# Attention beside a feed-forward network: the value products of a unit in one step or in two

## The chip, the cores and the metric

One core of one Trainium2 chip runs the whole program. The metric is the device time of one execution in microseconds. The engines are TensorE (PE, its weight loads PEld), VectorE (DVE), ScalarE (ACT) and GpSimd (POOL); SyncE (SP) issues the transfers by DMA.

## The reference, cut to what matters

```python
def _attn_ref(q, k, v, proj):                 # q, k, v: 4 x 8 x 768 x 64, proj: 64 x 6
    q_bits = (np.einsum('bhsd,dk->bhsk', q, proj) > 0)
    k_bits = (np.einsum('bhsd,dk->bhsk', k, proj) > 0)
    ...                                        # 6 bits make a bucket number
    mask = q_bucket[:, :, :, None] == k_bucket[:, :, None, :]
    scores = np.where(mask, scale * np.matmul(q, k.transpose(0, 1, 3, 2)), -1e9)
    attn = np.exp(scores - np.max(scores, axis=-1, keepdims=True))
    attn = attn / (np.sum(attn, axis=-1, keepdims=True) + 1e-09)
    return np.matmul(attn, v)

def _moe_ref(x, w_in, w_out):                 # x: 3072 x 512, 512 -> 2048 -> 512
    h = x @ w_in
    g = h * np.clip(h + 3.0, 0.0, 6.0) / 6.0
    return g @ w_out
```

The heads' outputs, laid side by side, are the tokens x of the feed-forward network (FFN).

## The kernel before, in words

Every product of 32-bit numbers is made of products of a rounded high part (fp32r) and of what is left of it, the low part. A high part is a cast by ScalarE; its low part is a subtraction by VectorE or GpSimd.

**Attention** goes by *row tiles*: tile k (0 to 191) holds 128 queries of one head against its 768 keys, six tiles to a head. For each, PE makes the scores (`lead`, L387 and L389: two banks of 384), VectorE takes the row minimum of the negated scores (`lowest`, L396), ScalarE the exponential with its row sum (`exponential`, L408). Two tiles make a *unit* u (tiles 2u and 2u+1). Up to tile 101 the probabilities are transposed by PE. From tile 102 (`GT`) on VectorE turns them inside blocks (`flip`, L429), a transfer writes them to DRAM (`fd<-p`), and four loads bring them back turned, two into a tile named `spare` and two into `px` (`move`, for tile k+1 at the end of step k; SP issues them). Then `split_p(k - 1, c)` makes the high part of a half c in tile ph and the low part in tile pl: ScalarE's cast L475 for both halves, GpSimd's subtraction L477 for c = 1, VectorE's L479 for c = 0. Row w = 0 of a unit's four tiles (ph and pl of c = 1 and of c = 0) is written in the odd step behind the tile, row w = 1 in the even step after. Tags ph and pl have two buffers each, and a unit takes both. The **value products** of a unit are twelve matmuls of 128x256 into one PSUM bank `acc`: six with the high parts, six with the low parts, of c = 1 first. `values_whole` (L513) makes them all at the start of an odd step. `output` then copies acc to a tile y (ScalarE, L547) in the next even step.

**The FFN** goes by chunks of 256 tokens, 16 places to a chunk, one place to a step. A generator `fill` makes it and is taken up four times in a step: A splits the gate's result (ScalarE's cast L689 and VectorE's L690), B makes the first layer (L661: eight products with x's high parts xh, four with its low parts xl), C makes the second layer of the place before (L699, L700, and as last the third terms L704, which need L690's result) and the gate (ScalarE L683, VectorE L684), D does side work: the reciprocals of the row sums (VectorE L567), the spreading of them (GpSimd L577), normalising transposes on PE (L587, into banks named rt), and at place 15 the split of the next chunk's x (L650 on ScalarE, L651 on VectorE).

**The hash** of a head ahead (`hash_qk`, L334 to L336) multiplies its queries and keys (high parts qq and kk, their low parts made by GpSimd in L318, which wait in a list `subs`; the transfers of the split wait in `moves`) into two PSUM banks z. VectorE reads the bits off them (`bits`, L352). Banks for z, h, acc and rt come from `bank`, in turn out of four.

The order on PE, VectorE, ScalarE and GpSimd is the order in which the code issues (a manual schedule); DMAs stand on SP's queue in that order too. From step 101 on one function, `beside_ffn`, writes a step. Its step k, before the change: in odd steps the value products of unit (k-3)/2; row minimum of tile k+2 (behind stage A where a hash was made in the step before); A; exponential and flip of tile k+2; split_p(k-1, 1); B; in even steps the copy of acc; in odd steps with (k+3) % 6 == 4 the hash of the next head; C, with split_p(k-1, 0) inside it; bits; scores of tile k+3; transfers; one low part of q or k from `subs` in odd steps; D.

Line numbers are those of the kernel before. In the changed kernel, lines from 516 on stand 15 lower for the parts named here (L661 becomes L676, L690 becomes L705, L547 becomes L562, L587 becomes L602), and L513 is in the new function `values_part`.

## Time and profile before

| | us |
|---|---|
| three runs | 974.35, 977.39, 976.26; median 976.26 |
| the profiled execution | 973.11, of it 971.3 in the span of the profile |
| mean granted clock of TensorE | 0.998 |
| busy share of the span | PE 98%, DVE 74%, ACT 64%, POOL 49% |
| stage 0 to 396 us: attention alone, row tiles 0 to about 100, weights split beside it | PE busy 385.3 of 396.0 |
| stage 396 to 813 us: attention beside the FFN, steps 101 to 192 | PE busy 410.2 of 417.0 |
| stage 813 to 971.3 us: the rest of the FFN | PE busy 152.6 of 158.3 |

Times are read from one profiled execution. A group's row gives line, engine, operation, output and input tiles, shape and count, then the busy time of all and the mean of one in ns, then the engine's idle time just before them and what ended most of it. A row of instructions in time gives start, duration, engine, line, tiles and (in brackets) the idle time in front and what ended it. A row by windows gives the stretch, its length and the busy time (and count) of PE, PEld, DVE, ACT and POOL, the granted clock, the share of the DMA engines and GB/s. Weight loads overlap the products; starts of PE's instructions are therefore better read than their ends.

### The profile page before, as it was taken

How to read it: one execution, taken by the hardware profiler on the slowest of the kernel's cores; microseconds unless marked ns; L12 is line 12 of the kernel's file. 1: busy time of each engine (PE TensorE's matmuls, PEld its weight loads, DVE VectorE, ACT ScalarE, POOL GpSimd, SP SyncE). 2: the span in 40 equal slices, each digit the busy share in tenths (PEclk: the TensorE clock that was granted, in tenths of full speed). 3: DMA queues.
4: the chain of work that ended last, by engine and by line, in shares of the span. 5: the costliest groups of instructions: out<-in, count | busy, mean ns of one | idle time of the engine just before them, and what ended most of it. 6: DMA issues, size and time to landing. Idle time of an engine off the chain costs nothing.

```text
span 971.3 us, 19460 instructions
## 1 busy us (share of the span) xinstructions
PE 948.0 (98%) x6306; PEld 873.6 (90%) x6306; DVE 723.5 (74%) x1470; ACT 625.0 (64%) x1421; POOL 473.6 (49%) x582
## 2 busy tenths in 40 slices
PE   8999999999999999899999999999999999999997
PEld 7999888999989999799899899989899899889896
DVE  7999988888569999877878878878777874342422
ACT  6898875655478988667766666666666664333332
POOL 6777744665537776455555545555545432000000
PEclk9999999999999999999999999999999999999999
DMA  3567579100035554787898788788887772101000
GB/s 117 140 156 188 131 224 377 58 1 1 6 119 119 115 142 112 192 252 233 238 267 234 231 256 241 230 267 236 243 258 233 211 227 71 44 1 44 1 22 22
DMA packets 113613, 152.06 MB, mean 157 GB/s; under 512 B 13876, under 2 KB 82612, under 8 KB 113512
## 3 DMA queue, kind: packets, MB, share of 16 engines
q1 hardware_dynamic: 108472, 144.79, 48.8%
q0 software_dynamic: 5040, 6.03, 5.3%
q8 instruction: 50, 0.82, 0.4%
q14 instruction: 51, 0.42, 0.2%
HBM read 77.34 MB, written 54.00 MB: 135 GB/s over the span
## 4 chain that ended last, share of the span: by engine, by line
PE 79%; DVE 8%; DMA 4%; ACT 4%; issue 3%; POOL 1%; SPq 1%; ACTq 0%; DVEq 0%; POOLq 0%
PE h L661 25%; PE acc L500 6%; PE po L704 6%; PE po L699 6%; PE po L700 6%; PE acc L513 6%; PE pt L418 5%; PE s L389 5%; PE s L387 5%; DMA spare<-fd 2%; DVE p L396 2%; DVE pl L479 2%; ACT ph L475 1%; SPq L78 1%; DVE qq L352 1%
## 5 line engine op out<-in xcount | busy, mean ns | idle before, releaser
L408 ACT ACTIVATE p<-p,m 128x768 f32<-128x768 f32 x192 | 180.2, 939 | 113.4 <-DVE p L396 105.2
L396 DVE TENSOR_SCALAR_CACHE_REDUCE p<-s 128x768 f32<-128x768 f32 x192 | 182.7, 952 | 24.9 <-PE pt L418 12.4
L684 DVE SCALAR_TENSOR_TENSOR h<-g,h 128x256 f32<-128x256 f32 x192 | 81.1, 423 | 102.0 <-ACT g L683 99.0
L683 ACT ACTIVATE g<-h,three 128x256 f32<-128x256 f32 x192 | 91.2, 475 | 94.9 <-PE h L661 94.0
L661 PE MATMUL h<-xh,w 128*128 128x256 f32 x1024 | 146.8, 282 | 0.0
L661 PEld LDWEIGHTS h<-xh,w 128*128 128x128 f32 x1024 | 134.9, 188 | 4.2 <-ACT xh L650 0.6
L429 DVE STREAM_TRANSPOSE p<-p 128x768 f32<-128x768 f32 x90 | 88.1, 979 | 65.2 <-ACT p L408 65.1
L477 POOL TENSOR_TENSOR pl<-spare,ph 128x384 fp32r<-128x384 f32 x45 | 45.8, 1018 | 127.3 <-ACT ph L475 71.4
L479 DVE TENSOR_TENSOR pl<-pt,ph 128x384 fp32r<-128x384 f32 x196 | 100.0, 550 | 4.0 <-ACT ph L475 3.5
L387 PE MATMUL s<-kk,qq 76*128 76x384 f32 x384 | 100.5, 343 | 2.0 <-ACT kk L357 1.5
L389 PE MATMUL s<-kk,qq 128*128 128x384 f32 x384 | 100.4, 343 | 0.0
L700 PE MATMUL po<-w,gb 128*128 128x512 f32 x250 | 98.4, 393 | 0.0
L699 PE MATMUL po<-w,gb 128*128 128x512 f32 x250 | 98.3, 393 | 0.0
L475 ACT CAST ph<-pt 128x384 fp32r<-128x384 f32 x196 | 86.1, 474 | 14.3 <-PE pt L418 13.0
L216 POOL TENSOR_TENSOR w<-wr,w 128x128 fp32r<-128x128 f32 x128 | 71.9, 593 | 45.2 <-ACT w L210 41.9
L418 PE MATMUL pt<-ident,p 128*128 128x128 f32 x612 | 86.2, 275 | 1.9 <-DVE pl L479 1.1
L689 ACT CAST gb<-h 128x256 fp32r<-128x256 f32 x141 | 52.4, 372 | 54.5 <-DVE h L684 26.8
L661 PE MATMUL h<-xl,w 128*128 128x256 f32 x512 | 81.2, 280 | 0.0
L418 PEld LDWEIGHTS pt<-ident,p 128*128 128x128 f32 x612 | 72.5, 141 | 8.9 <-PE pt L418 1.5
L704 PE MATMUL po<-w,gb 128*128 128x512 f32 x250 | 78.6, 395 | 1.5 <-DVE gb L690 1.5
L318 POOL TENSOR_TENSOR kk<-raw,qq 64x192 fp32r<-64x192 f32 (+1 forms) x73 | 65.4, 920 | 25.1 <-ACT qq L304 21.7
L387 PEld LDWEIGHTS s<-kk,qq 76*128 76x128 f32 x384 | 66.6, 190 | 11.7 <-ACT kk L357 2.0
(153 smaller groups left out, 2150.9 us busy)
## 6 DMA issues: line engine op xcount, KB each, us to landing
fd<-p SPq DMA_DIRECT2D x90, 384.0 KB
spare<-fd SPq DMA_DIRECT2D x180, 96.0 KB
px<-fd SPq DMA_DIRECT2D x180, 96.0 KB
kk<-qq SPq DMA_DIRECT2D x62, 192.0 KB
wr<-in_w_in SPq DMA_DIRECT2D x16, 512.0 KB
wr<-in_w_out SPq DMA_DIRECT2D x16, 512.0 KB
raw<-in_qkT SPq DMA_DIRECT2D x19, 384.0 KB
vr<-in_v SPq DMA_DIRECT2D x32, 192.0 KB
```

The source lines that it names most:

```text
L387: nc.tensor.matmul(s[:, c, :HW], lhsT=q1[:KM, us], rhs=half(k1[:KM], c), start=True, stop=False)
L389: nc.tensor.matmul(s[:, c, :HW], lhsT=q2[:, us], rhs=half(k2, c), start=False, stop=True)
L396: nc.vector.tensor_scalar(out=pr_[:], in0=s[:, :, :HW], scalar1=CAP, scalar2=None, op0=ALU.min, op1=ALU.min, accum_out=m[:],)
L408: nc.scalar.activation(pr_[:], pr_[:], AF.Exp, bias=m[:], scale=-1.0, accum_out=sms[b][:, t, h : h + 1])
L418: nc.tensor.transpose(pt[:, x], probs[g][0][:, c, x * P : (x + 1) * P], ident[:])
L475: nc.scalar.copy(hi, pt)
L479: lows.append(lambda: engine.tensor_sub(lo, pt, hi.bitcast(F32)))
L661: nc.tensor.matmul(hp, lhsT=wi[:, wp, wc], rhs=x[cc][xp], start=(k == 0 and cc == 0), stop=(k == 2 and cc == NCC - 1),)
L683: nc.scalar.activation(r[:], hp, AF.Relu, bias=three[:], scale=1.0)
L699: nc.tensor.matmul(po[u], lhsT=gh[:, us], rhs=wo[:, 0], start=(fc == 0), stop=False)
L700: nc.tensor.matmul(po[u], lhsT=gh[:, us], rhs=wo[:, 1], start=False, stop=False)
L704: nc.tensor.matmul(po[u], lhsT=gl[:, us], rhs=wo[:, 0], start=False, stop=(fc == NFC - 1))
```

## The change

The six high-part products of a unit stay in its odd step k, but stand behind the first layer (stage B); the six low-part products stand at the start of step k+1. The copy of acc stays in step k+1 at its place. The hash moves to the step before, an even one ((k+3) % 6 == 3), and whatever waits in `subs` and `moves` is issued ahead of it; `behind` follows it. A low part of q or k may now be issued in every step but those at place 15. The tiles, their buffers and the arithmetic stay.

```diff
+    def values_part(u: int, part: int):
+        vv = vvs[2 * u // KT]
+        if part == 0:
+            accs[u] = bank([P, 2 * P], f"acc{u}")
+        acc = accs[u]
+        for c in (1, 0):
+            y = parts[u, c][part]
+            for x in range(QT):
+                nc.tensor.matmul(
+                    acc[:], lhsT=vv[:, c * QT + x], rhs=y[:, x],
+                    start=(part, c, x) == (0, 1, 0), stop=(part, c, x) == (1, 0, QT - 1),
+                )
+            if part:
+                del parts[u, c]
...
+    begun_unit = None
+
+    def value_part(k: int, part: int):
+        nonlocal vnext, begun_unit
+        u = vnext // 2
+        if part == 0 and u < NS // 2 and 2 * u >= GT and k % 2 and k >= 2 * u + 3:
+            values_part(u, 0)
+            begun_unit = u
+        elif part == 1 and begun_unit is not None:
+            values_part(begun_unit, 1)
+            through.append(begun_unit)
+            begun_unit = None
+            vnext += 2
...
-                if u < NS // 2 and (2 * u < GT or k % 2 and k >= 2 * u + 3):
+                if 2 * u < GT:
...
-            behind = (k - 1 + LA) % KT == 4
+            value_part(k, 1)
+            behind = (k - 1 + LA) % KT == 3
...
             go("B")
+            value_part(k, 0)
...
-            hashed = k + LA < NS and (k + LA) % KT == 4 and (k + LA) // KT + 1 < NJ
+            hashed = k >= GT and k + LA < NS and (k + LA) % KT == 3 and (k + LA) // KT + 1 < NJ
             if hashed:
+                while subs:
+                    subs.pop(0)()
+                while moves:
+                    moves.pop(0)()
                 hash_qk((k + LA) // KT + 1)
...
-            if subs and (k % 2 and (k < GT or place_in_chunk != NFC - 1) or k > GT and place_in_chunk == 0):
+            if subs and (k < GT or place_in_chunk != NFC - 1):
                 subs.pop(0)()
```

What this makes of the order on the engines is shown at three places. In the rows a tile's name carries the unit or tile number (s128 are the scores of row tile 128, ph62_0 the high parts of unit 62, half c = 0) and last a running number of its buffer; "x3" is the count, and "PE_49" in a list of waits is a counter that the engine named raises.

PE, from the odd step 125 into the even step 126, with the products of unit 61 (acc61). Before:

```order
L513 MATMUL acc61_6979<-ph61_1_6883,vv20_6795 128x256 x3
L513 MATMUL acc61_6979<-ph61_0_6909,vv20_6795 128x256 x3
L513 MATMUL acc61_6979<-pl61_1_6884,vv20_6795 128x256 x3
L513 MATMUL acc61_6979<-pl61_0_6910,vv20_6795 128x256 x3
L661 MATMUL h1_1_7_7006<-xh1_1_6546,w14_2678 128x256 x8
L661 MATMUL h1_1_7_7006<-xl1_1_6547,w14_2678 128x256 x4
...
L704 MATMUL po1_1_6590<-w13_2644,gb1_1_6_6995 128x512 x2
L387 MATMUL s128_7032<-kk_21_6533,qq_21_6534 128x384 x2
L389 MATMUL s128_7032<-kk_21_6533,qq_21_6534 128x384 x2
L661 MATMUL h1_1_8_7058<-xh1_1_6546,w16_2777 128x256 x8
```

The same place after:

```order
L676 MATMUL h1_1_7_6997<-xl1_1_6541,w14_2678 128x256 x4
L513 MATMUL acc61_7010<-ph61_1_6870,vv20_6790 128x256 x3
L513 MATMUL acc61_7010<-ph61_0_6903,vv20_6790 128x256 x3
...
L719 MATMUL po1_1_6590<-w13_2644,gb1_1_6_6986 128x512 x2
L387 MATMUL s128_7030<-kk_21_6527,qq_21_6528 128x384 x2
L389 MATMUL s128_7030<-kk_21_6527,qq_21_6528 128x384 x2
L513 MATMUL acc61_7010<-pl61_1_6871,vv20_6790 128x256 x3
L513 MATMUL acc61_7010<-pl61_0_6904,vv20_6790 128x256 x3
L676 MATMUL h1_1_8_7058<-xh1_1_6540,w16_2777 128x256 x8
```

The high products have passed behind the first layer of their step; the low products have passed the first layer, the second layer and the scores s128, and stand in the next step.

VectorE, in the same odd step, around the low part of row 0 of the next unit (pl62_0). Before:

```order
L684 SCALAR_TENSOR_TENSOR h1_1_7_7006<-g1_1_7_7025,h1_1_7_7006 128x256 [waits Activation_49]
L479 TENSOR_TENSOR pl62_0_7029<-spare_5091,ph62_0_7028 128x3x128 [waits DMAHW1_49,DMAHW0_49,DMAHW5_49,DVE_49,DMAHW7_49,PE_49,Activation_49]
L396 TENSOR_SCALAR p128_7047,m128_7046<-s128_7032 128x768 [waits DMAHW3_49,PE_49]
L690 TENSOR_TENSOR gb1_1_7_7049<-h1_1_7_7006,gb1_1_7_7049 128x256 [waits Activation_49]
L429 STREAM_TRANSPOSE p128_7047<-p128_7047 128x768 [waits Activation_49]
```

After:

```order
L699 SCALAR_TENSOR_TENSOR h1_1_7_6997<-g1_1_7_7023,h1_1_7_6997 128x256 [waits Activation_49]
L479 TENSOR_TENSOR pl62_0_7027<-spare_5091,ph62_0_7026 128x3x128 [waits DMAHW1_49,DMAHW0_49,DMAHW6_49,DVE_49,DMAHW7_49,PE_49,Activation_49]
L396 TENSOR_SCALAR p128_7047,m128_7046<-s128_7030 128x768 [waits DMAHW3_49]
L705 TENSOR_TENSOR gb1_1_7_7049<-h1_1_7_6997,gb1_1_7_7049 128x256 [waits Activation_49]
L429 STREAM_TRANSPOSE p128_7047<-p128_7047 128x768 [waits Activation_49]
```

The order is the same. L479 waits for PE in both, for the last reader of the two pl buffers: before, that is the last low product of unit 61 at the start of the same step 125; after, the last one in step 126, which stands behind the scores s128. The row minimum behind it has lost its own wait for PE, since the count that L479 waits for is already past s128.

PE, the hash of head 20 (z20). Before, in the odd step 115:

```order
L661 MATMUL h1_0_13_6370<-xh1_0_5536,w26_3210 128x256 x8
L661 MATMUL h1_0_13_6370<-xl1_0_5537,w26_3210 128x256 x4
L334 MATMUL z20_0_6383<-qq_20_6144,pjl_74 108x384 [waits DVE_49]
L335 MATMUL z20_0_6383<-kk_20_6143,pjh_75 108x384 [waits DMAHW2_49]
L336 MATMUL z20_0_6383<-qq_20_6144,pjh_75 108x384 [waits DMAHW6_49]
L334 MATMUL z20_1_6384<-qq_20_6144,pjl_74 108x384 [waits DVE_49]
```

After, in the even step 114:

```order
L513 MATMUL acc55_6246<-pl55_1_6099,vv18_6018 128x256 x3
L513 MATMUL acc55_6246<-pl55_0_6132,vv18_6018 128x256 x3
L676 MATMUL h1_0_12_6300<-xh1_0_5536,w24_3141 128x256 x8
L676 MATMUL h1_0_12_6300<-xl1_0_5537,w24_3141 128x256 x4
L334 MATMUL z20_0_6315<-qq_20_6138,pjl_74 108x384 [waits DVE_49]
L335 MATMUL z20_0_6315<-kk_20_6137,pjh_75 108x384 [waits DMAHW1_49]
L336 MATMUL z20_0_6315<-qq_20_6138,pjh_75 108x384 [waits DMAHW6_49]
L334 MATMUL z20_1_6316<-qq_20_6138,pjl_74 108x384 [waits Activation_49]
```

The hash stands behind the low products and the first layer of an even step. Its first half waits for L705 of the step, and its second half for ScalarE, which there is the copy of acc55 to y (L562) that comes first in that bank; both waited for VectorE before.

## The prediction

> **What bounds the kernel now.** I read the page first, then the span by stage, then the groups of the value products, then instructions in order of time through two steps.

> ```profile
> span 971.3 us, 19460 instructions
> PE 948.0 (98%) x6306; PEld 873.6 (90%) x6306; DVE 723.5 (74%) x1470; ACT 625.0 (64%) x1421; POOL 473.6 (49%) x582
> PE 79%; DVE 8%; DMA 4%; ACT 4%; issue 3%; POOL 1%; SPq 1%; ACTq 0%; DVEq 0%; POOLq 0%
> ```

> ```profile
> 0.00:396.00 396.00, 385.31 (x2666) 358.88 (x2667) 340.78 (x708) 295.52 (x649) 253.96 (x294) 1.00 0.46 125
> 396.00:813.00 417.00, 410.18 (x2663) 377.92 (x2662) 326.65 (x625) 275.44 (x646) 213.12 (x274) 1.00 0.81 238
> 813.00:971.30 158.30, 152.55 (x982) 136.80 (x980) 56.11 (x138) 54.04 (x127) 6.48 (x14) 1.00 0.07 22
> ```

> TensorE is busy for 98% of the span and carries 79% of the chain that ended last. The stage that the change touches (attention beside the FFN) lies from 396 to 813 us; there PE is busy for 410 of 417 us. So time is won or lost only where PE stops or is slowed. Most of what it loses there it loses at the value products:

> ```profile
> L513 PE MATMUL acc<-ph,vv 128*128 128x256 f32 x276 | 44.9, 291 | 5.0 <-ACT ph L475 4.5
> ```

> ```profile
> 396.00:813.00 417.00, 79.29 (x552) 72.62 (x552) 1.00 0.81 238
> ```

> The last row is the busy time of L513 alone, 46 units of 12 products. The next rows are one even step (702.32 to 705.82) and the odd step behind it, a hash step.

> ```profile
> 702.16 2.07 SPq L78 DMA_DIRECT2D spare<-fd  x4
> 702.32 1.10 PE L661 MATMUL h<-xh,w 128*128 128x256 f32 x8
> 702.52 0.96 DVE L396 TENSOR_SCALAR_CACHE_REDUCE p<-s 128x768 f32<-128x768 f32 x1 [0.43 <-PE s L389]
> 703.40 0.42 DVE L690 TENSOR_TENSOR gb<-h,gb 128x256 fp32r<-128x256 f32 x1
> 703.52 0.94 ACT L408 ACTIVATE p<-p,m 128x768 f32<-128x768 f32 x1 [1.34 <-DVE p L396]
> 703.72 0.39 PE L699 MATMUL po<-w,gb 128*128 128x512 f32 x1
> 704.45 0.50 ACT L475 CAST ph<-px 128x384 fp32r<-128x384 f32 x1
> 704.64 0.63 PE L704 MATMUL po<-w,gb 128*128 128x512 f32 x2
> 704.86 0.36 ACT L547 COPY y<-acc 128x256 f32<-128x256 f32 x1
> 705.11 0.52 PE L387 MATMUL s<-kk,qq 76*128 76x384 f32 x2
> 705.12 0.47 ACT L683 ACTIVATE g<-h,three 128x256 f32<-128x256 f32 x1
> 705.49 0.51 ACT L475 CAST ph<-px 128x384 fp32r<-128x384 f32 x1
> 705.82 0.88 PE L513 MATMUL acc<-ph,vv 128*128 128x256 f32 x6
> 706.03 0.56 DVE L479 TENSOR_TENSOR pl<-px,ph 128x384 fp32r<-128x384 f32 x1
> 706.50 0.95 DVE L396 TENSOR_SCALAR_CACHE_REDUCE p<-s 128x768 f32<-128x768 f32 x1
> 706.53 0.88 PE L513 MATMUL acc<-pl,vv 128*128 128x256 f32 x6
> 707.25 1.10 PE L661 MATMUL h<-xh,w 128*128 128x256 f32 x8
> 708.43 0.50 ACT L475 CAST ph<-spare 128x384 fp32r<-128x384 f32 x1
> 708.66 0.34 PE L334 MATMUL z<-qq,pjl 128*108 128x384 f32 x1
> 709.70 0.40 PE L699 MATMUL po<-w,gb 128*128 128x512 f32 x1
> ```

> From the starts: first layer 1.40 us (702.32 to 703.72), second layer 1.39, its third terms 0.92 after its start (704.64), scores 0.71, high products 0.71, low products 0.72, hash 1.04. These are PE's slots, back to back. VectorE's row minimum (L396) starts 0.2 after the scores' last slot and sets off ScalarE's chain: exponential +1.00, high copy +0.93, copy of acc +0.41, gate +0.26, second high copy +0.37 for 0.51, VectorE's low subtraction (L479) right after, next minimum 0.47 on. Where that copy comes late, the value products stop:

> ```profile
> 567.38 0.51 ACT L475 CAST ph<-px 128x384 fp32r<-128x384 f32 x1
> 568.40 0.88 PE L513 MATMUL acc<-pl,vv 128*128 128x256 f32 x6
> ```

> The copy ends at 567.89; the low products start at 568.40, 0.51 later, where three slots are 0.36. So a stop costs its wait, 0.05 of signalling and about 0.10 until PE streams again.

> **What goes.** An unstopped unit keeps PE busy from 705.82 to 707.41 (706.53 + 0.88): 1.59. 46 units would be 73.1; L513 shows 79.3, 6.2 more, and stood idle for 5.0 in front. **11.2 us** is what ScalarE's late copies cost. Behind the first layer the high products come 1.40 later than the copies were late by in most units, and the low ones a step later still: I let all 11.2 go. It cannot be much more: PE's work is only moved, and the stage has 7 us of idle PE in all beside the slowed units.

> **What comes.** Two buffers carry tag ph and two tag pl, both taken by one unit. Step k (odd) writes row 0 of the next unit into them, ahead of the unit's own high products, and its low products come in step k+1. That the counts waited for are those of these products stands in the built program; what the waits last I lay out from the rows. In each odd step, then, ScalarE's high copies wait for high products of the same step, and GpSimd's and VectorE's low subtractions (L477, L479) wait for low products of step k+1. Behind VectorE's L479 stand the next minimum, the gate's subtraction (L690) and the rest of VectorE; ScalarE's exponential waits for the minimum.

> Call T the end of the low products' slots in the even step. L479 can start at T+0.19 (as the minimum after scores: 702.52 against 702.32). From L479's start to the next instruction VectorE takes 0.47 (706.03 to 706.50) when GpSimd is idle and 0.65 (590.16 to 590.81, below) beside it; nearer the second, I take 0.60, and the minimum starts at T+0.79; before it started at 0.2 after the scores, T-0.51. From the offsets above: L690 from T+1.67 to 2.09, exponential T+1.79, copy of acc T+3.13 to 3.49, second high copy done at T+4.27, next minimum T+4.77, L690 to T+6.07. PE: first layer to T+1.40, third terms of the second T+2.32 (need L690: 0.2 to spare), end T+3.50; odd step: high products at T+4.90 (copy done), third terms T+6.53 (0.4 to spare), low products end at T+8.43. ScalarE's second copy in the odd step ends about T+8.0. ScalarE's first high copy of the odd step stands behind the exponential and starts at T+6.70, when the high products it waits for have long passed (T+5.3). Behind GpSimd's held L477 stand the split of v, the adding DMAs and the low parts of q and k; the split is used two steps later, the rest is in item 4. So an ordinary pair costs nothing: PE's 8.43 is the longer loop. Where VectorE has more to do, or PE needs something sooner, it does:

> 1. Hash, now in even steps, 13 of them after the first. The hash takes PSUM banks in a ring of four. In 9 its second half waits for the L690 of the odd step: T+2.14 against T+1.40+0.52: 0.22 each, **2.0**. In 4 (steps 114, 132, 162, 180, where normalising transposes turn the ring) its second half waits for the copy of acc: T+3.56 against 1.92, **6.6**.

> ```profile
> 590.16 0.72 DVE L479 TENSOR_TENSOR pl<-spare,ph 128x384 fp32r<-128x384 f32 x1
> 590.81 0.57 DVE L567 TENSOR_SCALAR rc<-sms 128x16 f32<-128x16 f32 x1
> 591.58 0.90 DVE L396 TENSOR_SCALAR_CACHE_REDUCE p<-s 128x768 f32<-128x768 f32 x1
> ```

> ```profile
> 471.38 1.43 DVE L651 TENSOR_TENSOR xl<-xr,xh 128x256 fp32r<-128x256 f32 x4 [0.23 <-ACT xh L650]
> 472.73 0.95 DVE L396 TENSOR_SCALAR_CACHE_REDUCE p<-s 128x768 f32<-128x768 f32 x1
> ```

> ```profile
> 471.40 1.78 PE L661 MATMUL h<-xh,w 128*128 128x256 f32 x8
> 473.49 0.39 PE L699 MATMUL po<-w,gb 128*128 128x512 f32 x1
> ```

> ```profile
> 589.46 1.02 POOL L477 TENSOR_TENSOR pl<-spare,ph 128x384 fp32r<-128x384 f32 x1 [2.91 <-DMA kk<-qq]
> 590.55 2.47 POOL L318 TENSOR_TENSOR qq<-raw,qq 64x192 fp32r<-64x192 f32 x4
> ```

> 2. The row-sum reciprocals stand behind L479 in five odd steps: 0.77 (590.81 to 591.58). The minimum moves to T+1.56, L690 to T+2.86, third terms wait 0.59; four times 2.4, and once in a hash step 0.8: **3.1**.
> 3. At five chunk changes the four low parts of x (L651) stand behind L479, 1.35 for four (471.38 to 472.73). The first layer needs the last at its twelfth product; it comes at T+2.23, 1.0 late, and the minimum behind it costs another 0.3. Before, 0.7 was lost at 471.40 (2.09 to 473.49 against 1.40) and less elsewhere; I count 0.45 as already there: 5 x 0.85 = **4.3**.
> 4. GpSimd's L477 (1.02) starts at T-0.15. Where one of the head's two low parts (2.47) is still due, in 2 heads, the hash's second half gets it at T+3.34 against 2.27: with the 0.22 above, **1.7**. In 3 odd steps such a part also stands ahead of the spread copy for the normalising transposes: T+3.81 against 3.50, **0.9**.
> 5. Restarting, about 27 stops of 0.10: **2.7**.

> The flushing of moves and subs ahead of the hash issues no more than before; SP's queue is priced among the rivals. Sum: 2.0 + 6.6 + 3.1 + 4.3 + 1.7 + 0.9 + 2.7 = 21.3, less 11.2: **+10.1 us**. The profiled execution took 973.1 (span 971.3), 3.2 under the median of 976.3; added to the median, 986.4: I say **986**.

> The unknown in it is where the minimum starts. If L479 takes its short 0.56 beside a free GpSimd and all waits come 0.1 early, items 1 to 3 lose about 2.3 together per 0.1 us; if 0.2 later, every even step's third terms lose their 0.2 and 27 ordinary pairs start to pay. That gives 979 to 996 for this case.

> **Rivals.** *VectorE is hardly held.* Place: L479 in odd steps. If its minimum starts near T+0.2, as an L479 finished before T would allow, only item 1's wait for acc (4 x 1.05), item 4 and some 2 us of the rest stay, about 8 against 11.2: 973, or 970 without item 4. It turns into a gain from about T+0.3 on. For it: ScalarE's copy in front may itself be late, so that the old order of late and early engines returns; against it: the low products lie 0.7 after the scores in program order, and the subtraction cannot pass them.

> *The two sides cancel*: gains of 11 and stops of 8 to 14, 973.4 to 979.2. This is the first case with the minimum 0.2 to 0.4 earlier.

> *GpSimd and VectorE collide.* Both subtractions are now released within 0.35 us of each other. In the rows above GpSimd's runs from 589.46 to 590.48 and VectorE's from 590.16, and that one takes 0.72 where 706.03 takes 0.56: slowed, not shut out. Shut out, L479 would start at T+0.87 and the minimum at T+1.45: third terms 0.4 late in 27 even steps (10.8) and 0.66 more in some 20 places of items 1 to 3 (13): 1010. [...]

> *SP's queue.* The loads of spare wait for both subtractions: they were issued at 702.16, 0.16 before the scores ended, and used at 708.43; now they go out at about T+0.95 and are used at about T+6.7, 5.8 us instead of 6.3. If that falls short by 0.3 in each of 45 odd steps, 13 us more: 999.

> **Chances.** First case 0.55 (979 to 996), cancelling 0.14, VectorE hardly held 0.19, collision or SP's queue 0.12. A measurement of this kernel tells from no change about 0.3%, 2.9 us: faster 0.19, same 0.14, slower 0.67. The range 970 to 999 leaves out the outer halves of the last two.

> **What would show it.** ScalarE's wait no longer in front of the value products; VectorE's L479 waiting for PE's low products in odd steps, some 0.5 us each; the minimum 0.8 after the low products; PE waiting for the copy of acc in four hash steps, for L690 in hash and reciprocal steps, for the low parts of x at chunk changes; 27 or so stops, none in ordinary pairs. I am wrong if PE runs through the hash steps, or if ordinary pairs stop as well.

## The result, and the profile after

Five runs of the changed kernel took 1017.01 to 1021.15 us, median 1020.97, against 976.26 before: a ratio of 1.0449, with a 95% interval of 1.0424 to 1.0474. Ratios below are to the kernel before, too, with the same kind of interval. It is 45 us slower, on the forecast side but more than four times the forecast of 10, and outside the range of 970 to 999.

The profile after, from the same places of the page as before (span, busy shares, the chain by engine), of an execution of 1021.03 us:

```profile
span 1019.3 us, 19417 instructions
PE 971.9 (95%) x6306; PEld 877.3 (86%) x6306; DVE 749.4 (74%) x1470; ACT 623.0 (61%) x1421; POOL 475.6 (47%) x582
PE 72%; DVE 16%; DMA 4%; issue 2%; ACT 2%; POOL 2%; SPq 1%; DVEq 0%; ACTq 0%; POOLq 0%
```

VectorE's share of the chain has doubled, 8% to 16%. By stage, with a last stretch of the same length as before (158.3 us):

```profile
396.00:861.00 465.00, 435.52 (x2671) 383.25 (x2670) 352.03 (x626) 274.45 (x649) 215.46 (x275) 0.97 0.73 213
861.00:1019.30 158.30, 152.47 (x981) 136.67 (x979) 56.14 (x138) 53.77 (x127) 6.49 (x14) 0.99 0.07 22
```

The whole 48 us lie in the stage that was changed: 465.0 us against 417.0, and the tail's PE time is what it was. A new number stands there: the granted clock is 0.97 over the stage. Groups that wait now (after), and VectorE's held subtraction as it was before:

```profile
L479 DVE TENSOR_TENSOR pl<-spare,ph 128x384 fp32r<-128x384 f32 x45 | 50.2, 1115 | 29.3 <-PE acc L513 14.5 <-DMA fd<-p 7.9 <-DMA px<-fd 5.0
L719 PE MATMUL po<-w,gb 128*128 128x512 f32 x250 | 85.7, 425 | 7.3 <-DVE gb L705 7.0
L676 PE MATMUL h<-xl,w 128*128 128x256 f32 x512 | 83.5, 282 | 3.9 <-DVE xl L666 3.9
L334 PE MATMUL z<-qq,pjl 128*108 128x384 f32 x64 | 23.1, 361 | 11.2 <-DVE gb L705 8.7 <-ACT y L562 2.5
L562 ACT COPY y<-acc 128x256 f32<-128x256 f32 x92 | 33.9, 369 | 13.7 <-PE acc L500 6.8 <-DMA xs<-y 3.6 <-PE acc L513 1.4
```

```profile
L479 DVE TENSOR_TENSOR pl<-spare,ph 128x384 fp32r<-128x384 f32 x45 | 29.4, 653 | 0.6 <-DMA px<-fd 0.2 <-DVE h L684 0.2
```

VectorE's 45 subtractions for row 0 wait 29.3 us (0.6 before), as the change made them, but each also lasts 1.12 us instead of 0.65, which was not expected. Behind them stand third terms (L719) waiting 7.0 us for L705, low parts of x 3.9, the hash 8.7 for L705 and 2.5 for the copy of acc. The copy of acc itself waits 3.6 us for a DMA.

An ordinary pair in order of time: the end of an odd step (scores, low products from 601.78) and the even step behind it.

```profile
601.78 0.88 PE L513 MATMUL acc<-pl,vv 128*128 128x256 f32 x6
602.43 1.02 POOL L477 TENSOR_TENSOR pl<-spare,ph 128x384 fp32r<-128x384 f32 x1 [4.00 <-DMA px<-fd]
602.49 1.10 PE L676 MATMUL h<-xh,w 128*128 128x256 f32 x8
602.75 1.11 DVE L479 TENSOR_TENSOR pl<-spare,ph 128x384 fp32r<-128x384 f32 x1 [0.50 <-PE acc L513]
603.78 0.94 DVE L396 TENSOR_SCALAR_CACHE_REDUCE p<-s 128x768 f32<-128x768 f32 x1
604.66 0.41 DVE L705 TENSOR_TENSOR gb<-h,gb 128x256 fp32r<-128x256 f32 x1
605.13 0.73 PE L719 MATMUL po<-w,gb 128*128 128x512 f32 x2 [0.16 <-DVE gb L705]
```

T, the end of the low products' slots, is 602.49. L479 starts at T+0.26 (forecast T+0.19), but the minimum only at T+1.29 (forecast T+0.79): 1.03 us behind L479's start instead of 0.60. GpSimd's L477 had started 0.32 earlier and ended at 603.45; L479 ended at 603.86, 0.41 later. So L705 ends at 605.07, and the third terms, due at about 604.8, stop. In 32 of 42 pairs of the stage the minimum starts at T+1.29 to 1.39; in the others reciprocals or low parts of x stand ahead of it.

A hash step of the four in which the ring is turned, and then by windows (the third figure from the end is the granted clock) the stretch with its stops and the one behind:

```profile
455.00 0.95 PE L513 MATMUL acc<-pl,vv 128*128 128x256 f32 x6
456.05 1.12 DVE L479 TENSOR_TENSOR pl<-spare,ph 128x384 fp32r<-128x384 f32 x1 [0.71 <-PE acc L513]
457.09 0.94 DVE L396 TENSOR_SCALAR_CACHE_REDUCE p<-s 128x768 f32<-128x768 f32 x1
457.96 0.41 DVE L705 TENSOR_TENSOR gb<-h,gb 128x256 fp32r<-128x256 f32 x1
458.43 0.42 PE L334 MATMUL z<-qq,pjl 128*108 128x384 f32 x1 [1.08 <-DVE gb L705]
459.41 0.36 ACT L562 COPY y<-acc 128x256 f32<-128x256 f32 x1
459.83 0.42 PE L334 MATMUL z<-qq,pjl 128*108 128x384 f32 x1 [0.62 <-ACT y L562]
460.79 0.63 PE L715 MATMUL po<-w,gb 128*128 128x512 f32 x1
```

```profile
457.00:460.50 3.50, 1.81 (x11) 1.25 (x10) 3.00 (x7) 2.42 (x6) 1.34 (x2) 1.00 0.73 224
460.50:464.00 3.50, 3.50 (x11) 2.92 (x10) 2.36 (x5) 0.42 (x2) 0.10 (x1) 0.51 0.76 225
```

The first half of the hash stops for L705, the second for the copy of acc, 1.24 and 0.78 us beyond the slots. Right behind, PE is busy all the time but at a clock of 0.51: a 512-wide product takes 0.43 us from start to start (460.79 to 461.22) where 0.23 is its slot. In the kernel before, this stage shows nothing of the kind; its granted clock is 1.00.

To add up, PE's time was taken from start to start of its products, less the slot of their kind (0.118 us for 256 columns, 0.178 for 384, 0.233 for 512), and summed by what was waited for; slots near 1.8 times their length (0.21 for 256 columns, 0.43 for 512), four or more in a row, are the halved clock. In us of the changed stage, for the two kernels and for two experiments below:

| PE's time beyond its slots | before | after | vector_first | vf_xl_add |
|---|---|---|---|---|
| value products | 7.4 | 3.0 | 4.2 | 0.9 |
| hash | 0.3 | 16.0 | 8.3 | 9.9 |
| third terms and second layer | 1.9 | 14.1 | 5.8 | 7.1 |
| low parts of x at chunk changes | 0.3 | 6.9 | 6.7 | 0.4 |
| first layer | 1.8 | 4.1 | 4.8 | 3.3 |
| normalising transposes | 0 | 0 | 2.8 | 2.4 |
| halved clock | 0 | 8.9 | 3.6 | 0 |
| pieces under 0.13 (restarts) | 7.1 | 12.4 | 8.5 | 8.0 |
| sum with the small rest | 17.3 | 64.3 | 43.8 | 31.1 |

The small rest is about 1 us below zero in each column: products a little shorter than their slot. The sum grew by 47.0 us, the span by 48.0.

### The profile page after: what moved, and what is told of

Its sections match the earlier page's. It is cut to its first block, busy times and chain, and to the rows that moved or that the text cites. A ratio compares the mean times of both kernels' runs of the same rounds, so it can differ in the third digit from the quotient of the medians.

```text
span 1019.3 us, 19417 instructions
## 1 busy us (share of the span) xinstructions
PE 971.9 (95%) x6306; PEld 877.3 (86%) x6306; DVE 749.4 (74%) x1470; ACT 623.0 (61%) x1421; POOL 475.6 (47%) x582
## 4 chain that ended last, share of the span: by engine, by line
PE 72%; DVE 16%; DMA 4%; issue 2%; ACT 2%; POOL 2%; SPq 1%; DVEq 0%; ACTq 0%; POOLq 0%
PE h L676 20%; PE po L719 7%; DVE pl L479 6%; PE acc L500 6%; PE po L714 5%; PE po L715 5%; DVE p L396 5%; PE s L389 5%; PE s L387 5%; PE pt L418 5%; PE acc L513 5%; DMA px<-fd 2%; DVE gb L705 1%; SPq L78 1%; PE z L334 1%
## 5 line engine op out<-in xcount | busy, mean ns | idle before, releaser
L408 ACT ACTIVATE p<-p,m 128x768 f32<-128x768 f32 x192 | 180.1, 938 | 170.4 <-DVE p L396 162.2
L396 DVE TENSOR_SCALAR_CACHE_REDUCE p<-s 128x768 f32<-128x768 f32 x192 | 182.2, 949 | 16.5 <-PE pt L418 11.6
L699 DVE SCALAR_TENSOR_TENSOR h<-g,h 128x256 f32<-128x256 f32 x192 | 81.0, 422 | 100.7 <-ACT g L698 97.9
L477 POOL TENSOR_TENSOR pl<-spare,ph 128x384 fp32r<-128x384 f32 x45 | 45.7, 1015 | 182.2 <-DMA px<-fd 83.0
L387 PE MATMUL s<-kk,qq 76*128 76x384 f32 x384 | 102.2, 347 | 2.0 <-ACT kk L357 1.5
L479 DVE TENSOR_TENSOR pl<-pt,ph 128x384 fp32r<-128x384 f32 x196 | 100.0, 550 | 4.0 <-ACT ph L475 3.5
L714 PE MATMUL po<-w,gb 128*128 128x512 f32 x250 | 101.0, 404 | 0.7 <-ACT gb L704 0.7
L389 PE MATMUL s<-kk,qq 128*128 128x384 f32 x384 | 101.6, 346 | 0.0
L715 PE MATMUL po<-w,gb 128*128 128x512 f32 x250 | 100.9, 403 | 0.0
L475 ACT CAST ph<-pt 128x384 fp32r<-128x384 f32 x196 | 85.9, 473 | 14.0 <-PE pt L418 12.7
L719 PE MATMUL po<-w,gb 128*128 128x512 f32 x250 | 85.7, 425 | 7.3 <-DVE gb L705 7.0
L676 PE MATMUL h<-xl,w 128*128 128x256 f32 x512 | 83.5, 282 | 3.9 <-DVE xl L666 3.9
L704 ACT CAST gb<-h 128x256 fp32r<-128x256 f32 x141 | 52.4, 371 | 48.6 <-DVE h L699 33.3
L387 PEld LDWEIGHTS s<-kk,qq 76*128 76x128 f32 x384 | 68.4, 195 | 12.4 <-ACT kk L357 2.1
L318 POOL TENSOR_TENSOR kk<-raw,qq 64x192 fp32r<-64x192 f32 (+1 forms) x73 | 67.6, 950 | 18.9 <-ACT qq L304 16.5
```

The source lines that it names most:

```text
L387: nc.tensor.matmul(s[:, c, :HW], lhsT=q1[:KM, us], rhs=half(k1[:KM], c), start=True, stop=False)
L389: nc.tensor.matmul(s[:, c, :HW], lhsT=q2[:, us], rhs=half(k2, c), start=False, stop=True)
L396: nc.vector.tensor_scalar(out=pr_[:], in0=s[:, :, :HW], scalar1=CAP, scalar2=None, op0=ALU.min, op1=ALU.min, accum_out=m[:],)
L408: nc.scalar.activation(pr_[:], pr_[:], AF.Exp, bias=m[:], scale=-1.0, accum_out=sms[b][:, t, h : h + 1])
L479: lows.append(lambda: engine.tensor_sub(lo, pt, hi.bitcast(F32)))
L676: nc.tensor.matmul(hp, lhsT=wi[:, wp, wc], rhs=x[cc][xp], start=(k == 0 and cc == 0), stop=(k == 2 and cc == NCC - 1),)
```

## The experiments

Three theories are named in what was put on record. *Lock*: GpSimd's L477, released first, keeps VectorE's L479 from reading. *Hold*: the wait for the low products is the cost by itself. *Hash*: its even place is the cost.

### Does the collision cost it? gp_behind, gp_behind_late, vector_first

gp_behind: GpSimd starts behind VectorE, with a copy of two elements of VectorE's result (`ends`) ahead of its subtraction.

```diff
-        if engine is nc.gpsimd:
+        if engine is nc.gpsimd and w == 0 and paced:
+            gps.append(lambda: engine.tensor_sub(lo, pt, hi.bitcast(F32)))
+        elif engine is nc.gpsimd:
             engine.tensor_sub(lo, pt, hi.bitcast(F32))
...
     def split_lows():
         for f in lows:
             f()
         lows.clear()
+        if ends:
...
+            nc.gpsimd.tensor_copy(tiny[:], ends.pop().bitcast(F32))
+            gps.pop()()
```

> The changed kernel, with GpSimd's subtraction for row 0 (L477 in odd steps) held until VectorE's (L479) is done, by a copy of two elements of VectorE's result ahead of it on GpSimd; nothing else is moved. Lock theory (most of the 45 us come because GpSimd's L477, released 0.3 us ahead, keeps VectorE's L479 from reading until it ends): L479 in even steps takes 0.56 instead of 1.12, the row minimum starts at T+0.75 instead of T+1.30, the third terms of the ordinary even steps no longer wait (0.32 before, 0.42 with the restart), each wait of hash, reciprocal and chunk-change steps gets 0.55 shorter, some of the halved-clock stretches go: 986 to 996 us. Hold theory (the wait for the low products itself is the cost, whoever else reads): L479 is no faster to matter, 1012 us or more. Hash theory (the hash's two waits in even steps and the halved clock behind them are the cost): 1005 to 1015.

1008.1 us (1.0337, 1.0319 to 1.0356): 13 us back, not 25 to 35; by its time it lies in the range of the hash theory. The lock theory's mechanism came as expected, its time did not:

```profile
L483 DVE TENSOR_TENSOR pl<-spare,ph 128x384 fp32r<-128x384 f32 x45 | 25.2, 560 | 23.5 <-PE acc L521 9.5 <-DMA px<-fd 6.7 <-ACT gb L712 4.6
L610 PE MATMUL rt<-ident,spare 128*128 128x128 f32 x72 | 14.3, 281 | 7.4 <-POOL spare L600 6.3 <-ACT y L570 1.1
```

VectorE's subtraction (L483 here) takes 0.56, the minimum starts at T+0.37 to 0.48 in 28 of 42 pairs, and third terms, hash and halved clock lose 20 us less together by the count above. But GpSimd is now late with what stands behind its subtraction: transposes wait 6.3 us for the spread copy, and 2.6 us more go at the value products, mostly where the copy of acc waits for the adding DMA. The edit also does more than was meant: VectorE's subtraction is now issued first and so gets the buffer that is freed first, as in vector_first below. It starts at T-0.10 to T+0.00 in most pairs instead of T+0.26, so 0.26 of the earlier minimum is not the collision's. The same holds for gp_behind_late.

gp_behind_late puts the same subtraction behind that work, into the next step, and with it the loads of spare that wait for its reading.

```diff
             if GT <= k < NS - 2 and behind:
                 lowest(k + 2)
+            if ends:
...
+                nc.gpsimd.tensor_copy(tiny[:], ends.pop().bitcast(F32))
+                gps.pop()()
+            if k > GT and k % 2 == 0 and k < NS:
+                move(k)
```

> The lock alone, without the new lateness of gp_behind (1008.1 us, where spread copies and adding DMAs stood behind the later L477): GpSimd's subtraction for row 0 is put into the next step, behind the other work of its odd step, and there still waits for VectorE's L479, which stays at its place and stays held by the low products. Lock theory: L479 0.56 us long, the minimum at T+0.47, transposes no longer late; 985 to 996 us, some 25 to 35 of the 45 us back. Hold theory: 1008 or more.

1006.0 us (1.0322, 1.0295 to 1.0349). The transposes' wait for the spread copy is down to 1.0 and the subtraction takes 0.58, but ScalarE's first copy in odd steps now waits 22.5 us for the loads of spare, and the hash for L705 behind it. The time lies between the ranges of both theories, so this kernel did not tell them apart by it.

vector_first exchanges only who gets which buffer: the first of the two pl tiles that is written takes the buffer freed first. No engine's order changes.

```diff
+        if engine is nc.gpsimd and w == 0 and g > GT:
+            gps.append(lambda: engine.tensor_sub(lo, pt, hi.bitcast(F32)))
...
     def split_lows():
         for f in lows:
             f()
+        if lows and gps:
+            gps.pop()()
         lows.clear()
```

> The changed kernel, with the order of the first writes into the two pl buffers exchanged in odd steps (VectorE's subtraction is issued ahead of GpSimd's; no engine's own order changes). VectorE's L479 so takes the buffer that the third low product frees, 0.36 us ahead of the sixth, and GpSimd's L477 the other. [...] Hold theory (only the 0.36 counts, at 50 us for 1 us as low_early had it: 36 us for 0.71): 1000 to 1006.

1000.2 us (1.0245, 1.0226 to 1.0264): 20.8 us back. A pair of it:

```profile
618.98 0.96 PE L517 MATMUL acc<-pl,vv 128*128 128x256 f32 x6
619.77 0.56 DVE L481 TENSOR_TENSOR pl<-spare,ph 128x384 fp32r<-128x384 f32 x1 [0.20 <-issue]
620.07 1.13 POOL L477 TENSOR_TENSOR pl<-spare,ph 128x384 fp32r<-128x384 f32 x1 [3.54 <-PE acc L517]
620.24 0.95 DVE L396 TENSOR_SCALAR_CACHE_REDUCE p<-s 128x768 f32<-128x768 f32 x1
622.10 0.63 PE L723 MATMUL po<-w,gb 128*128 128x512 f32 x2
```

With T at 619.77, VectorE starts at T+0.00 and the minimum at T+0.47, 0.83 earlier than after the change: 0.26 of that is the earlier buffer, 0.56 the collision. GpSimd, second now, takes 1.13. The third terms of ordinary pairs don't stop. So the collision is shown as a mechanism, and it is the larger part of 0.83. By its time the kernel lies at the lower end of the hold theory's 1000 to 1006, and above the 978 to 990 of the lock theory: GpSimd's subtraction starts 0.36 later, with the adding DMA and the spread copies behind it, and the chunk changes kept their 6.7 us. vf_xl_add below takes two of these waits away.

### Does the hold cost it? low_early, early_vector_first, early_vf_xl

low_early releases both engines 0.71 us sooner.

```diff
-            value_part(k, 1)
             behind = (k - 1 + LA) % KT == 3
...
+            value_part(k, 1)
             if k + LA < NS:
                 lead(k + LA)
```

> The changed kernel, with the six low products ahead of the scores of the odd step instead of behind them (0.71 us earlier against the rest of PE's work). Lock and hold theory: L479 is released 0.7 us earlier, still takes 1.12 beside GpSimd's L477, and the minimum starts 0.6 after the scores (before the change 0.2): third terms wait in no ordinary step, the hash's waits shrink by 0.7 a half, at chunk changes about 0.6 stays: 972 to 984 us. Hash theory: 1000 or more, since the hash stays where it is.

985.1 us (1.0104, 1.0085 to 1.0122), 1 us above the range of lock and hold theory, and 36 of the 45 us back with the collision left in: VectorE's subtraction still takes 0.96 on average. That speaks against the hash theory (the hash's wait for L705 falls from 8.7 to 0.9 us with the hash where it is), and shows how steep the cost is: 36 us for 0.71 us. The queues of both engines are earlier with it, and the granted clock of the execution is 1.00.

early_vector_first adds the exchange of vector_first, in the same lines.

> low_early (985.1 us) and vector_first together: the low products ahead of the scores, and VectorE's subtraction first. Lock theory: the minimum again starts 0.2 to 0.3 after the scores as before the change; what is left is the hash's wait for the copy of acc in four steps (3 to 4 us), some of GpSimd's lateness, and the gain of about 10 us at the value products: 972 to 980 us. Hold theory: no better than low_early, 983 or more.

992.0 us (1.0172, 1.0157 to 1.0188): worse than low_early. By its words the hold theory had that (no better, 983 or more), but the trace shows a reason that neither theory had. The low products now end before ScalarE's second copy does, so VectorE can't use its earlier buffer, while GpSimd can start:

```profile
667.29 0.87 PE L517 MATMUL acc<-pl,vv 128*128 128x256 f32 x6
667.87 0.50 ACT L475 CAST ph<-spare 128x384 fp32r<-128x384 f32 x1
668.30 1.01 POOL L477 TENSOR_TENSOR pl<-spare,ph 128x384 fp32r<-128x384 f32 x1 [5.36 <-DMA px<-fd]
668.46 1.26 DVE L481 TENSOR_TENSOR pl<-spare,ph 128x384 fp32r<-128x384 f32 x1
669.64 0.94 DVE L396 TENSOR_SCALAR_CACHE_REDUCE p<-s 128x768 f32<-128x768 f32 x1
```

T is 668.00, ScalarE's copy ends at 668.37. VectorE comes 0.16 after GpSimd and ends 0.41 after it (669.72, 669.31). It is the collision again, with the other engine's lead decided by ScalarE.

early_vf_xl puts the low parts of x ahead of the held subtraction at place 15.

```diff
...
             go("D")
+            if k > GT and place_in_chunk == NFC - 1:
+                split_lows()
+                if GT <= k + 1 < NS:
+                    move(k + 1)
```

> early_vector_first, and at the five chunk changes (place 15) VectorE's held subtraction is put behind the low parts of x instead of ahead of them. Lock and hold theory: what is left at chunk changes (4.6 us in low_early) goes; 2 to 5 us below early_vector_first. Rival: the loads of spare behind the later subtraction come late; no better, or up to 4 us worse.

989.3 us (1.0144, 1.0129 to 1.0159), 2.7 below; the low parts of x stop PE no longer.

### Can the held work be put off? low_late, both_late, both_late_hash_old

low_late makes row 0's low part on VectorE behind the next step's minimum and L705.

```diff
-                amid.append(lambda: (split_p(k - LT, 0, False), split_lows()))
+                amid.append(lambda: (split_p(k - LT, 0, False), None if k % 2 else split_lows()))
...
             if GT <= k < NS - 2 and behind:
                 lowest(k + 2)
+            if k > GT:
+                split_lows()
+                if k % 2 == 0 and k < NS:
+                    move(k)
...
```

> The changed kernel, with VectorE's subtraction for row 0 (L479 of odd steps) behind the next step's row minimum and gate subtraction, and the loads of the next tile into spare behind it; PE's order is that of the change. Lock and hold theory alike: nothing that PE waits for stands behind the held subtraction any more; the minimum starts 0.2 after the scores as before the change, the waits of hash, third terms and chunk changes go, and what is left is the gain that was forecast for the value products: 963 to 970 us. Hash theory: the hash's waits for the copy of acc stay, 975 to 1000. If loading spare about 5 us ahead of its use is too late, ScalarE's first copy of odd steps waits for the transfer: 975 to 990.

982.6 us (1.008, 1.0057 to 1.0103): the best version here, and short of the 963 to 970. It lies in the range that was given for loads of spare that come too late (975 to 990), which the row of low_late below bears out; the hash theory's 975 to 1000 holds it as well. both_late puts GpSimd's part behind too, and both_late_hash_old takes the hash back to odd steps.

```diff
             if k > GT:
                 split_lows()
+                if gps:
+                    gps.pop()()
...
-            behind = (k - 1 + LA) % KT == 3
+            behind = (k - 1 + LA) % KT == 4
...
-            hashed = k >= GT and k + LA < NS and (k + LA) % KT == 3 and (k + LA) // KT + 1 < NJ
+            hashed = k + LA < NS and (k + LA) % KT == 4 and (k + LA) // KT + 1 < NJ
```

The first two lines with a plus are both_late, with GpSimd's subtraction set aside as in vector_first; the rest, with the old popping of `subs` and no flush, is added in both_late_hash_old.

> As low_late (982.6 us), and GpSimd's subtraction for row 0 (L477 of odd steps) is put into the next step too, behind the splits of v, the low parts of q and k, the spread copies and the adding DMAs of its odd step. Held-engines theory (what low_late still loses over the value products' gain is GpSimd's held queue: transposes waiting for the spread copy 3.8 us, the hash for low parts of q and k 2.7, ScalarE's copy of acc for the adding DMA 3.3 with 1.4 to 2 of halved clock): 968 to 975 us, and these three waits are gone. Rival (the even place of the hash with its turn of banks costs it, whatever GpSimd does): 979 to 985.

> As both_late, with the hash and the low parts of q and k back at their old places in odd steps. Held-engines theory: no more than 3 us from both_late, 965 to 974 us. Rival (the even place of the hash): 8 us or more faster than both_late.

995.5 us (1.0205, 1.0187 to 1.0223) and 992.7 (1.0174, 1.0148 to 1.0199). Both are worse than low_late, against the ranges of both theories. The hash's place makes 2.8 us in time, about as much as the runs of one kernel differ, and that is no clean measure of it: with the hash in odd steps its wait for VectorE goes from 11.5 to 1.3 us, but the second layer then waits 12.8 us for ScalarE's part of the gate's split. ScalarE's first copies of low_late and of both_late, which waited 1.4 us before the change:

```profile
L475 ACT CAST ph<-spare 128x384 fp32r<-128x384 f32 x90 | 45.3, 503 | 14.2 <-DMA spare<-fd 8.1 <-PE po L719 3.1 <-PE acc L513 3.0
```

```profile
L475 ACT CAST ph<-spare 128x384 fp32r<-128x384 f32 x90 | 45.3, 504 | 41.8 <-DMA spare<-fd 36.1 <-PE z L336 3.8 <-PE acc L515 1.1
```

The loads of the next tile go into the tile that the subtraction reads. Whoever puts the reading off puts the loads off: 8.1 us of waiting for them in low_late, 36.1 in both_late. That is the last rival of the prediction, of which the changed kernel itself shows nothing (ScalarE waits 1.7 us for these loads).

### The hash alone: hash_only

The kernel before with these lines of the change and the emptying of `subs` and `moves` ahead of the hash, and value products whole:

```diff
-            behind = (k - 1 + LA) % KT == 4
+            behind = (k - 1 + LA) % KT == 3
...
-            hashed = k + LA < NS and (k + LA) % KT == 4 and (k + LA) // KT + 1 < NJ
+            hashed = k >= GT and k + LA < NS and (k + LA) % KT == 3 and (k + LA) // KT + 1 < NJ
...
-            if subs and (k % 2 and (k < GT or place_in_chunk != NFC - 1) or k > GT and place_in_chunk == 0):
+            if subs and (k < GT or place_in_chunk != NFC - 1):
```

> The kernel before, with the hash alone moved to the even step (and the low parts of q and k issued as in the change); the value products stay whole at the start of odd steps. Lock and hold theory: the hash finds its banks free in time, since nothing holds VectorE; 974 to 980 us. Hash theory: a good part of the 45 us is here, 990 or more.

988.8 us (1.0136, 1.0111 to 1.0161), nearly what the hash theory had.

```profile
L334 PE MATMUL z<-qq,pjl 128*108 128x384 f32 x64 | 23.2, 363 | 9.4 <-ACT y L547 9.0
```

With whole value products at the start of odd steps, acc takes its bank ahead of the odd step's h, and the even hash's second half comes to acc's bank in nine steps, not four: 9.0 us of waiting for its copy, against 2.5 in the changed kernel. So this is not the hash's share in the changed kernel, where the products' new place turns the ring; it is a cost of its own of moving the hash without them. The opposite, the spread products with the hash left in odd steps, was not run. By the order of the code it can't be without putting the subtraction off: the hash would wait for L705, that for L479, that for low products that stand behind the hash.

### The halved clock by itself: stops

Idle reductions on VectorE, whose result nobody reads, before the gate's subtraction in the last batch of the kernel before.

```diff
+                if tail % 4 == 0 and tail // 4 <= len(STOPS):      # (6, 7, 8, 9, 10, 11, 12, 13, 14, 16, 9, 10)
+                    for _ in range(STOPS[tail // 4 - 1]):
...
+                        nc.vector.tensor_reduce(out=tiny[:], in_=g, op=ALU.max, axis=AX.X)
```

> The halved clock by itself: the kernel before, with 6 to 16 idle reductions of about 0.33 us on VectorE ahead of the gate's subtraction in every fourth place of batch 3's chunks, where VectorE has little to do and 1.4 us of slack. PE's third terms should stop there for about 0.5 to 3.8 us, one stop in some 11 us. If the clock falls by the sum of the stops within a short stretch, as the changed kernel has it (1.24 and 0.78 us within 2 us: halved for 3.1 us; 1.04 alone: not), PE's slots are 1.8 times as long for some 3 us behind stops of about 2 us and more, and not behind those of about 1 us. Rival: the halved clock belongs to the attention's kinds of work and doesn't show behind any of these stops, or behind every one.

One execution took 1027.5 us. PE stopped twelve times, for 1.0 to 5.6 us. The clock that the trace records is halved for 3.413 us at a time in the changed kernel, in stops also for longer (the 6.00 us from 950.00 are all at 0.50). These windows lie on one grid: the seven in the changed kernel's stage end at 463.92, 556.08, 569.73, 665.30, 713.09, 805.25 and 818.90 us, which are 27, 4, 28, 14, 27 and 4 times 3.413 apart. Here are windows of the grid of stops around a stop of 2.38 us (from 886.02), one of 2.40 (from 1001.59) and one of 3.55 (from 930.19):

```profile
884.37:887.79 3.42, 1.81 (x12) 1.28 (x10) 3.17 (x8) 0.48 (x1) 0.00 (x0) 1.00 0.00 0
887.79:891.20 3.41, 2.80 (x18) 2.58 (x19) 1.37 (x5) 1.94 (x4) 0.00 (x0) 1.00 0.01 3
1000.43:1003.84 3.41, 1.31 (x8) 0.80 (x6) 3.21 (x8) 0.48 (x1) 0.00 (x0) 1.00 0.00 0
1003.84:1007.25 3.41, 3.27 (x13) 3.07 (x14) 0.85 (x3) 0.37 (x1) 0.00 (x0) 0.50 0.00 0
928.75:932.16 3.41, 1.60 (x10) 1.09 (x9) 3.14 (x9) 0.00 (x0) 0.00 (x0) 1.00 0.00 0
932.16:935.57 3.41, 1.83 (x13) 1.70 (x14) 2.60 (x7) 1.02 (x3) 0.40 (x1) 1.00 0.00 0
```

The first stop lies across a border of the grid, with 1.77 us of it in one window, and the clock stayed. The second, as long, has 2.25 in one window, and the next window was halved. The third is cut into 1.97 and 1.58, and the clock stayed although it is longer than both. So here the sum of the stops decided, as expected, but within a window of this grid and not within any short stretch; in the changed kernel the 1.24 and 0.78 us of a hash step and two short restarts make 2.2 of one window (457.09 to 460.50). The rival falls: stops in the FFN alone halved the clock (0.50 from 1003.84), and of the first two, as long as each other, only the second did. Counted like this in all traces kept here (from 30 us on, from the slots above), 41 windows at full clock were followed by a halved one. In 39 of them PE stood, beyond its slots, for 2.04 us or more; in two, one in gp_behind_late and one in both_late, for 1.86. Of some 3900 windows that were not, none had more than 2.03. In the changed kernel alone the seven falls of its stage stand behind windows with 2.07 to 2.90 us, and its windows behind which the clock stayed had 1.93 at most.

### Two of the rest's waits taken away: vf_xl_add

vector_first, the reordering of early_vf_xl at place 15, and GpSimd's adding DMAs ahead of its held subtraction:

```diff
+            if k % KT in (1, 3):
+                add()
             if split:
                 split_p(k - LT, 1, False)
...
-            if k % KT in (1, 3):
-                add()
```

> vector_first (1000.2 us) with two waits of its rest taken away by order alone: at the five chunk changes VectorE's held subtraction stands behind the low parts of x, and GpSimd's adding DMAs stand ahead of its held subtraction in odd steps instead of behind it. If that rest is made of these stops as its trace shows them: the low parts of x give 6 us back (6.7 in the trace), ScalarE's wait for the adding DMA and the stop of PE behind it near 646 us give 4 to 6 with the halved clock: 988 to 991 us, and both waits are gone from the trace. Rival: GpSimd now waits at the adding DMA for the transfer before it, and its subtraction and the low parts of q and k behind it come late: 995 or more, with PE waiting in the hash for GpSimd.

986.6 us (1.0107, 1.0061 to 1.0154), 13.6 below vector_first and a little better than expected.

```profile
396.00:827.90 431.90, 415.25 (x2671) 376.06 (x2670) 330.13 (x626) 275.70 (x649) 213.84 (x276) 1.00 0.78 230
```

```profile
L481 DVE TENSOR_TENSOR pl<-spare,ph 128x384 fp32r<-128x384 f32 x45 | 25.8, 573 | 17.4 <-PE acc L517 6.2 <-ACT qq L304 3.2 <-ACT gb L708 3.2
L680 PE MATMUL h<-xl,w 128*128 128x256 f32 x512 | 81.3, 280 | 0.0
L566 ACT COPY y<-acc 128x256 f32<-128x256 f32 x92 | 34.0, 369 | 10.1 <-PE acc L504 6.8 <-PE acc L517 1.4
```

The low parts of x no longer stop PE, the copy of acc no longer waits for a DMA (5.1 us in vector_first), and the granted clock is 1.00: the table's halved clock has gone with the long stops, and no window of the grid has as much as 2 us of them left. 34 of the 45 us are back with PE's order untouched.

## Why the prediction was wrong, point by point

**What goes** was right in kind and too large. L513 and what stood in front lost 7.4 us in stops before and 3.0 after, 2.8 of which are one stop that was 1.7 long before (below); with the restarts among these products it is about 12 and 5. The forecast was 11.2; the trace gives about 7, or 8 without that one place, for not all of it went.

**The failing step** is in the layout: "From L479's start to the next instruction VectorE takes 0.47 when GpSimd is idle and 0.65 beside it; nearer the second, I take 0.60". It takes 1.03. The row for 0.65 had L479 come 0.70 us behind GpSimd's start, 0.32 before its end. That it then took 0.72 was read as slowing. It fits a lock as well: L479 ended 0.41 after GpSimd, and so it does in all 53 collisions of the changed kernel in which it came 0.14 to 0.69 behind GpSimd's start (0.41 to 0.43), and in early_vector_first. In the new place GpSimd has just begun, and nearly all of its 1.02 us are waited for. The trace of the kernel before already held rows that tell the two readings apart, where VectorE came sooner behind GpSimd:

```profile
558.42 1.01 POOL L477 TENSOR_TENSOR pl<-px,ph 128x384 fp32r<-128x384 f32 x1
558.80 1.06 DVE L479 TENSOR_TENSOR pl<-px,ph 128x384 fp32r<-128x384 f32 x1
```

L479 came 0.38 behind and took 1.06. The other way round it is the same: in vector_first GpSimd, coming 0.06 to 0.40 behind VectorE, took 1.38 to 1.04, always ending 0.86 to 0.88 after VectorE. In these rows each engine ends its own time (0.56 and 1.02) less about 0.15 after the other's end, whatever the overlap. "Shut out", as the rival had it, was the better reading, and the rows bear it out but for these 0.15: kept out to GpSimd's recorded end, L479 would have ended its own 0.56 after it, and it ended 0.41.

The rival got 0.12 together with another; its minimum at T+1.45 was 0.15 too late, its price of 10.8 us for 27 ordinary pairs compares with 20 stops of 0.32 and 0.10 for restarting behind, 8.4 us. The prediction's own scale bears the step out: a minimum at T+1.29, 0.50 later than in it, costs items 1 to 3 five times 2.3, 11.5, and the ordinary pairs 8.4, which makes +30 of its +10. The halved clock (8.9), which it had not priced, and the 4 us that did not go at the value products make about +43; measured were 45 to 48.

**Its consequences** by the items of the sum:

- Hash: 2.0 and 6.6, with 1.7 for GpSimd. Measured 16.0. Five of the nine lose 0.79, not 0.22, and two lose 1.2 each for GpSimd's low parts; the four lose 2.0 each, not 1.64.
- Reciprocals: 3.1. Four steps lose 1.04 or 0.94 at the third terms, 4.0, and the one in a hash step 0.3 more than its like.
- Chunk changes: 4.3 more. Measured 6.9 at the low parts of x where 0.3 stood.
- Ordinary pairs: "an ordinary pair costs nothing". This was the false sentence: 8.4.
- Restarts: 2.7. The small pieces grew by 5.3.

**What was left out.** First, the clock: 8.9 us in seven stretches: six behind two stops in quick succession (1.24 and 0.78 in four hash steps, 1.13 and 1.02 at two chunk changes), one behind a stop of 2.8. Second, the adding DMA: it was named behind GpSimd's held L477 and given no price. At one place it decides:

```profile
653.08 1.01 POOL L477 TENSOR_TENSOR pl<-spare,ph 128x384 fp32r<-128x384 f32 x1 [5.50 <-DMA px<-fd]
655.91 1.67 POOL L537 DMA_DIRECT2D xs<-y  x2
658.47 0.52 PE L513 MATMUL acc<-ph,vv 128*128 128x256 f32 x3
660.41 0.37 ACT L562 COPY y<-acc 128x256 f32<-128x256 f32 x1 [3.56 <-DMA xs<-y]
```

The copy of acc waits 3.6 us for the DMA that reads y's old content, behind it the high parts, and PE's high products stop for 2.8 us; 0.9 of stops and 1.0 of halved clock follow. In the kernel before, the same copy waited 1.1 and the same products stopped for 1.7.

What was on record to be looked for came mostly true (no ScalarE wait in front of the value products but at that one place, PE waiting for the copy of acc in four hash steps, for L705 in hash and reciprocal steps, for the low parts of x); "none in ordinary pairs" and "the minimum 0.8 after the low products" did not.

**What stays open.** vf_xl_add is still 12 us over before. By the table its hash and third terms hold 15 of that, against 6.5 gained at the value products, which is close to the old sum of +10, but no experiment undid these one by one. That the two numbers are close is in part luck: with the minimum at T+0.47 there, the prediction's scale would give about +3 and not +12. Its rows still show the hash waiting 2.9 us for the gate's subtraction, 2.8 for GpSimd's low parts and 2.5 for the copy of acc, and transposes 1.9 for the spread copy. Own buffers for ph and pl, which would end the hold itself, were not tried.

## What to carry to other kernels

When a matmul is put later, look for who writes its operands' buffers next: the wait moves to that engine, and everything in its queue pays, here 36 us for 0.71 us. If two engines are released by the same group, lay them out against each other to 0.1 us (here 0.32 between the starts made 1.11 us of a subtraction of 0.56), and read a collision by the end of the one against the end of the other (0.41 to 0.43 behind it in 53 collisions), not by how much it was lengthened. And price stops together that can fall into one window of the grid, 3.413 us here: each looks cheap, but where they came to 2.07 us or more of a window, 8.9 us of halved clock followed in all.
